# Three of the first expert's blocks ahead of a branch, the third block's halves, the low parts of weights and uncommon numbers behind it

## The chip, the cores and the metric

The kernel runs on one core of one Trainium2 chip. The engines named below are TensorE (PE; its weight loads are PEld), VectorE (DVE), ScalarE (ACT), GpSimd (POOL) and SyncE (SP, which issues most DMA transfers). A "q" behind a name (DVEq, SPq) is that engine's own instruction queue, which handles branches, semaphores and register loads. The metric is the device time of one execution in microseconds (us).

## The reference

Three stages run one after another on 4 x 768 = 3072 tokens of 384 numbers, all in float32:

```
# 1: gated linear attention, state 48 x 48 per head
state = alpha[t] * state + k[t] v[t]^T;   y[t] = q[t] @ state
# 2: mixture of 8 experts, one per token
expert = argmax(xn @ en.T / tau);   h = max(x @ w1[e], 0);   out = gate * (h @ w2[e])
# 3: dense layer pair
g = elu(x @ w_in);   out = g @ w_out          # 384 -> 2048 -> 384
```

## The kernel before

**Stages.** Attention goes over 24 tiles of 128 tokens. The tokens of each tile are scattered to rows of the table `xs` in memory, one region for each expert, by indirect transfers that POOL issues (`put`). The second stage then takes the experts one after another. Expert 0 always comes first; the order of the others is found from their token counts (`pack`, which also fills `perm_i`, `off_i` and so on). The rows of an expert come back by a transposing transfer (`load_rows`, tile `xr`), are joined to float32 (`join`, tile `xj`) and split (`evict`) into a high part `xh` (ACT) and a low part `xl` (DVE).

**One block.** Each expert has 8 blocks of 128 hidden units. `mm1(e, f)` is nine matmuls for the first layer (`h`, three products for each of three slices: high times high, low times high, high times low), then ACT writes the high half `hh` and DVE the low half `hl`. `mm2(e, f)` is nine matmuls for the second layer (`y`), one block later. `h` has 3 buffers in PSUM, `hh` and `hl` have 2 each, `y` has one set.

**Weights.** Raw weights arrive in pieces of 128 x 512 (`raw`, `load_w`, `fetch`). ACT writes the high part (`whi`) and DVE the low part (`wlo`, `low_part` in `split_piece`). Of the nine pieces taken during attention the last five low parts are postponed (list `spare`); two are done in attention and three in `rest_of`.

**The branch.** A number `odd_i` says whether the input is uncommon (too few tokens at some place, an overflow, a decay out of range). Every engine loads it and compares; in the common case all jump over a long repair path (`fix`, with `redo`, which writes the first expert's tiles again). At the place where the two paths meet each engine first waits for its own earlier work and then adds to its semaphores what the skipped path would have added. Whatever waits for that engine behind the branch waits for this addition.

**Order.** Around the branch the order of each engine is that of the code (`manual_schedule`); DVE, ACT and POOL take their instructions in that order. SP's queue holds, in order, the transposing transfer of the next expert's rows, raw weights, and the chain that brings the gate weights of an expert to all partitions (`load_g`: `rx`, `gd`, `gs`), which DVE needs when `y` of the expert is finished (line 1118).

Of the kernel before, what the change touches and what calls it, by code (L numbers as in the profile page):

```python
# [68 lines left out]
def fused_kernel(ctx, tc, qk, a, v, w12, wi, wo, cst, cols, out):  # L69
# [40 lines left out]
    en = const.tile([128, 1, E], F32, name="en")  # L110
    tick = const.tile([1, 1], F32, name="tick")
    mark = c["mark"].rearrange("p (n two) -> p n two", two=2)

# [58 lines left out]
    def load_w(n=1):  # L172

        for _ in range(n):
            if nload[0] < len(pieces):
                pool = early_p[0] if DIRECT <= nload[0] < AHEAD * PIECES else stage
# [112 lines left out]
    def attention(st):  # L289
        if True:  # L290
# [5 lines left out]
            sm = st.enter_context(tc.tile_pool(name="sm", bufs=2))  # L296
            early_p.append(st.enter_context(tc.tile_pool(name="early", bufs=AHEAD * PIECES - DIRECT)))
            psD = st.enter_context(tc.tile_pool(name="psD", bufs=2, space=PS))
# [383 lines left out]
            def fast():  # L682
# [55 lines left out]
                for i in range(tail):  # L738
# [14 lines left out]
                    stR(i + 2)  # L753
                    stA(i + 2)
                    if i == tail - 1:
                        late.pop(0)()
                        late.pop(0)()
                    stP(i + 1, 0)
                    stP(i + 1, 1)
# [78 lines left out]
            def ending():  # L838
# [83 lines left out]
                tests = pk[:9] + dec[12:] + pk[9:]  # L922
                tests, rest = tests[:len(tests) - 9], tests[len(tests) - 9:]
                for kk in range(KD):
                    first_x(GROUPS[g1], kk, stop=True)
                    nc.vector.tensor_tensor(xj[kk][:, W0:], t0[kk][:, W0:], xj[kk][:, W0:], op=ALU.add)
                    run(tests[:2])
                    del tests[:2]
# [22 lines left out]
            def fix(x2T, redo):  # L951
# [3 lines left out]
                with ExitStack() as st2:  # L955
                    ld = st2.enter_context(tc.tile_pool(name="ldF", bufs=3))
                    wk = st2.enter_context(tc.tile_pool(name="wkF", bufs=2))
                    xp = st2.enter_context(tc.tile_pool(name="xpF", bufs=10))
                    sm = st2.enter_context(tc.tile_pool(name="smF", bufs=2))
                    psD = st2.enter_context(tc.tile_pool(name="psDF", bufs=2, space=PS))  # L960
                    ps1 = st2.enter_context(tc.tile_pool(name="ps1F", bufs=1, space=PS))
                    bad = nc.values_load(bad_i[0:1, 0:1], min_val=0, max_val=C2 + 128)
                    with tc.If(bad > 0):
                        vt = [wk.tile([128, NP, 128], F32, bufs=1, name=f"vF{i}") for i in range(VB)]
                        with tc.manual_schedule():
                            general()
                            run(pack(sm, psT_p.tile([128, E], F32, tag="psT", name="n_ps")))
                    zero = xp.tile([128, XW], U16, tag="xt", name="zero")
# [17 lines left out]
    def pack(sm, n_ps):  # L986

        low_f, ov, co, m, one, cm = (sm.tile([1, E], F32, bufs=1, name=nm) for nm in ("low_f", "ov", "co", "m", "one", "cm"))
# [4 lines left out]
        val, by = (sm.tile([1, 2, E], F32, bufs=1, name=nm) for nm in ("val", "by"))  # L993
        sq, cn = [1, E, E], by[:, 1]
# [20 lines left out]
            lambda: vec.scalar_tensor_tensor(odd, odd, few, co[:, E - 1:E], op0=ALU.add, op1=ALU.add),  # L1015
            lambda: vec.tensor_tensor(odd_i, odd, bad_i, op=ALU.add),
            lambda: vec.tensor_copy(cnt_i, val[:, 1]),
            lambda: vec.tensor_copy(perm_i, by[:, 0]),
# [3 lines left out]
            lambda: vec.tensor_tensor_scan(cm, one, m, co[:, E - 1:E], op0=ALU.mult, op1=ALU.add),  # L1022
            lambda: vec.tensor_copy(over_i, co[:, E - 1:E]),
            lambda: vec.tensor_tensor(col_i, co, ov, op=ALU.subtract),
            lambda: vec.tensor_tensor(off_i, cm, m, op=ALU.subtract),
        ]

    def moe1(att, xr0, t0, rest_of, fix, es):
        with ExitStack() as st:
            xT_p = st.enter_context(tc.tile_pool(name="xT", bufs=2, side="right"))  # L1030
            h_p = st.enter_context(tc.tile_pool(name="h", bufs=2, side="right"))
            xr, xT, hb, acc, gs = {0: xr0}, {}, {}, {}, {}
            first, freed = [], []
# [24 lines left out]
            def load_g(e, f):  # L1058

                if f == (0 if e else EARLY):  # L1060
                    nc.sync.dma_start(out=rx[0:1, :CAPS[e]].rearrange("o (n u) -> o n u", u=1),
                                      in_=xs[bass.ds(expert(e) * REG, CAPS[e]), 2 * DM + 2:].bitcast(F32).rearrange("(o n) u -> o n u", o=1))
                if f == (2 if e else EARLY + 2):
                    nc.sync.dma_start(out=gd[e:e + 1, :CAPS[e]], in_=rx[0:1, :CAPS[e]])
                if f == (4 if e else EARLY + 3):
# [3 lines left out]
            def mm1(e, f, between=None):  # L1069
                hb[e, f] = (h_p.tile([128, CAP], F32R, tag="hh", name="hh"),  # L1070
                            h_p.tile([128, CAP], F32R, tag="hl", name="hl"))
                first_layer(psG.tile([128, CAP], F32, tag="g", name="h")[:, :CAPS[e]], e, f, between)

            def first_layer(ps, e, f, between=None):
                n = CAPS[e]
                xh, xl = (x[:, :, :n] for x in xT[e])
                for kk in range(KD):
# [4 lines left out]
                    if between and kk == 1:  # L1082
                        between()
                hh, hl = (h[:, :n] for h in hb[e, f])
                nc.scalar.activation(out=hh, in_=ps, func=AF.Relu)
                nc.vector.scalar_tensor_tensor(hl, ps, 0.0, hh.bitcast(F32), op0=ALU.max, op1=ALU.subtract)  # L1086

            def redo():

                with tc.tile_pool(name="psF", bufs=2, space=PS) as pool:  # L1090
                    for kk in range(KD):
                        x = xj_p.tile([128, CAP], F32, tag="xj", name="xj")
                        join(nc.gpsimd, x, xr0, kk, CAP)
                        evict(0, kk, x)
                    for f in range(EARLY):
                        first_layer(pool.tile([128, CAP], F32, name="h"), 0, f)

# [48 lines left out]
            with tc.manual_schedule():  # L1146
# [5 lines left out]
                for n in range(EARLY, len(blocks) + LAG):  # L1152
                    if n < len(blocks):
                        e, f = blocks[n]
                        mm1(e, f)
                        if n == EARLY:
                            mm2(*blocks[n - LAG - 1])
                        load_g(e, f)
                        joined(e + 1, f - (2 if e else 3))
                        turn(e + 1, f - 4)  # L1160
                    if n == len(blocks):
# [261 lines left out]
```

## Time and profile before

| | |
|---|---|
| time, median of 3 runs (lowest, highest) | 770.99 us (770.52, 771.67) |
| time of the profiled execution | 770.17 us |
| its span, first to last instruction | 768.5 us |
| PE busy | 749.3 us (98%) |
| DVE, ACT, POOL busy | 534.5, 354.6, 207.0 us |

The span is what the trace covers; the time has 1.7 us around it. All times of the trace count from the span's start. The branch stands at about 147 to 155 us, between attention and the experts.

### The profile page before, as it was taken

How to read it: one execution, taken by the hardware profiler on the slowest of the kernel's cores; microseconds unless marked ns; L12 is line 12 of the kernel's file. 1: busy time of each engine (PE TensorE's matmuls, PEld its weight loads, DVE VectorE, ACT ScalarE, POOL GpSimd, SP SyncE). 2: the span in 40 equal slices, each digit the busy share in tenths (PEclk: the TensorE clock that was granted, in tenths of full speed). 3: DMA queues.
4: the chain of work that ended last, by engine and by line, in shares of the span. 5: the costliest groups of instructions: out<-in, count | busy, mean ns of one | idle time of the engine just before them, and what ended most of it. 6: DMA issues, size and time to landing. Idle time of an engine off the chain costs nothing.

```text
span 768.5 us, 13502 instructions
## 1 busy us (share of the span) xinstructions
PE 749.3 (98%) x4982; PEld 685.8 (89%) x4982; DVE 534.5 (70%) x990; ACT 354.6 (46%) x733; POOL 207.0 (27%) x239
## 2 busy tenths in 40 slices
PE   8999999699999999999999999999999999999996
PEld 5888887599999999999888999999999999999996
DVE  8899999748998989995667655455554645545442
ACT  2565765455566566654455423333333323323221
POOL 7747687513443444440000100020020002002002
PEclk9999999999999999999999999999999999999998
DMA  8999963457976887750000000010010001001001
GB/s 199 249 269 264 240 183 115 131 123 220 247 188 214 242 223 229 220 175 11 0 2 1 22 21 0 1 42 1 0 42 1 1 0 42 2 1 41 1 1 41
DMA packets 64129, 76.92 MB, mean 100 GB/s; under 512 B 34580, under 2 KB 40604, under 8 KB 64060
## 3 DMA queue, kind: packets, MB, share of 16 engines
q1 hardware_dynamic: 60988, 66.57, 32.8%
q0 software_dynamic: 3072, 9.46, 3.4%
q8 instruction: 39, 0.64, 0.4%
q14 instruction: 30, 0.25, 0.1%
HBM read 58.78 MB, written 12.25 MB: 92 GB/s over the span
## 4 chain that ended last, share of the span: by engine, by line
PE 42%; issue 32%; DVE 3%; POOL 3%; ACT 0%; DMA 0%; POOLq 0%; DVEq 0%; ACTq 0%
PE h L1268 9%; PE y L1112 4%; PE y L1111 4%; PE y L1113 4%; PE h L1080 4%; PE h L1081 4%; PE h L1079 4%; PE o L1291 3%; PE o L1289 3%; PE o L1290 3%; POOL out_dram L1302 2%; DVE wlo L196 1%; DVE wd L232 0%; DVE hl L1086 0%; DVE xl L1102 0%
## 5 line engine op out<-in xcount | busy, mean ns | idle before, releaser
L1270 DVE TENSOR_SCALAR mn<-h 128x512 f32<-128x512 f32 x96 | 66.3, 691 | 144.4 <-PE h L1268 144.4
L1271 ACT ACTIVATE mn<-mn 128x512 f32<-128x512 f32 x96 | 60.7, 632 | 171.8 <-DVE mn L1270 171.7
L1291 PE MATMUL o<-dwo,gl 128*128 128x384 f32 x384 | 130.0, 339 | 0.0
L1290 PE MATMUL o<-dlo,gh 128*128 128x384 f32 x384 | 128.5, 335 | 0.0
L1289 PE MATMUL o<-dwo,gh 128*128 128x384 f32 x384 | 128.4, 334 | 0.0
L1268 PE MATMUL h<-xh,dlo 128*128 128x512 f32 x288 | 113.2, 393 | 0.0
L1268 PE MATMUL h<-xl,dwi 128*128 128x512 f32 x288 | 112.9, 392 | 0.0
L1268 PE MATMUL h<-xh,dwi 128*128 128x512 f32 x288 | 112.7, 391 | 0.0
L1302 POOL DMA_INDIRECT out_dram<-ob,ids x24 | 23.2, 965 | 332.3 <-ACT ob L1299 328.6
L1277 ACT ACTIVATE gh<-g 128x512 fp32r<-128x512 f32 x96 | 60.7, 633 | 77.7 <-DVE g L1274 77.7
L196 DVE TENSOR_TENSOR wlo<-raw,whi 128x512 fp32r<-128x512 f32 x96 | 72.6, 782 | 6.5 <-ACT whi L193 6.5
L1274 DVE SCALAR_TENSOR_TENSOR g<-mn,h 128x512 f32<-128x512 f32 x96 | 66.2, 689 | 15.4 <-ACT mn L1271 15.0
L1289 PEld LDWEIGHTS o<-dwo,gh 128*128 128x128 f32 x384 | 72.1, 188 | 4.1
L1290 PEld LDWEIGHTS o<-dlo,gh 128*128 128x128 f32 x384 | 72.1, 188 | 4.0
L1291 PEld LDWEIGHTS o<-dwo,gl 128*128 128x128 f32 x384 | 72.2, 188 | 1.5 <-DVE gl L1278 0.6
L1080 PE MATMUL h<-xl,whi 128*128 128x432 f32 (+6 forms) x192 | 67.3, 351 | 3.2 <-DVEq L1134 2.8
L1079 PE MATMUL h<-xh,whi 128*128 128x432 f32 (+6 forms) x192 | 67.0, 349 | 1.9 <-ACTq L1134 1.1
L1112 PE MATMUL y<-hl,whi 128*128 128x432 f32 (+6 forms) x192 | 67.2, 350 | 0.3 <-DVE hl L1086 0.3
L1081 PE MATMUL h<-xh,wlo 128*128 128x432 f32 (+6 forms) x192 | 66.9, 348 | 0.0
L1111 PE MATMUL y<-hh,whi 128*128 128x432 f32 (+6 forms) x192 | 66.7, 348 | 0.0
L1113 PE MATMUL y<-hh,wlo 128*128 128x432 f32 (+6 forms) x192 | 66.6, 347 | 0.0
L1278 DVE TENSOR_TENSOR gl<-g,gh 128x512 fp32r<-128x512 f32 x96 | 65.7, 685 | 1.1 <-ACT gh L1277 1.1
(214 smaller groups left out, 1416.8 us busy)
## 6 DMA issues: line engine op xcount, KB each, us to landing
raw<-in_w_dram SPq DMA_DIRECT2D x96, 256.0 KB
qk<-in_qk_dram SPq DMA_DIRECT2D x46, 192.0 KB
raw<-in_wi_dram SPq DMA_DIRECT2D x16, 384.0 KB
raw<-in_wo_dram SPq DMA_DIRECT2D x16, 384.0 KB
vt<-in_v_dram SPq DMA_DIRECT2D x24, 192.0 KB
at<-in_alpha_dram SPq DMA_DIRECT2D x40, 99.0 KB
xs<-zero SPq DMA_DIRECT2D x7, 289.5 KB
at<-in_alpha_dram SPq DMA_DIRECT2D x4, 231.0 KB
```

The costliest lines, as they stand in the source:

```text
L196: nc.vector.tensor_tensor(l[:, sl], r, h[:, sl].bitcast(F32), op=ALU.subtract)
L1079: nc.tensor.matmul(ps, wh, xh[:, kk], start=(kk == 0), stop=False)
L1080: nc.tensor.matmul(ps, wh, xl[:, kk], start=False, stop=False)
L1081: nc.tensor.matmul(ps, wl, xh[:, kk], start=False, stop=(kk == KD - 1))
L1111: nc.tensor.matmul(acc[e][d], wh, hh, start=(f == 0), stop=False)
L1112: nc.tensor.matmul(acc[e][d], wh, hl, start=False, stop=False)
L1113: nc.tensor.matmul(acc[e][d], wl, hh, start=False, stop=(f == FB - 1))
L1268: nc.tensor.matmul(ps, l, x, start=(n == 0), stop=(n == len(terms) - 1))
L1270: nc.vector.tensor_scalar(mn, ps, 0.0, None, op0=ALU.min)
L1289: nc.tensor.matmul(o_, gh[:, sl], wh, start=(f == 0), stop=False)
L1290: nc.tensor.matmul(o_, gh[:, sl], wl, start=False, stop=False)
L1291: nc.tensor.matmul(o_, gl[:, sl], wh, start=False, stop=(f == M - 1))
```

## The change

- Three blocks of expert 0 instead of two stand ahead of the branch (`EARLY = 3`). The third block's halves `hh` and `hl` come behind it (`mm1` is split into `products` and `mm1_end`), between `mm2` of block 0 and `mm2` of block 1.
- The three postponed low parts of weights (`split_spare`) and the three raw pieces of the next expert (`load_w`) move from ahead of the branch to behind it. The pieces that wait for them stay in the `stage` buffers, so the pool `early` shrinks from 5 to 2 buffers.
- Numbers that only the repair path reads (`cnt_i`, `size_i`, `slot_i`, `over_i`, `col_i`) are computed in the repair path by `pack_over`.
- In front of the branch, the chain for the last two tiles' gate weights (`n1`) comes before the tests that give `odd_i`, and fewer tests stand between the additions to `xj`.
- In attention, step 21, DVE does a reduction and a low part before the scan `stA`.
- The gate chain `load_g` of expert 0 starts one block later and is closer together; the joins and splits of the next expert's three slices come at blocks 4, 5, 5 and 5, 6, 6 instead of 3, 4, 5 and 4, 5, 6.

```diff
@@ attention, step loop
                     stR(i + 2)
-                    stA(i + 2)
                     if i == tail - 1:
                         late.pop(0)()
                         late.pop(0)()
+                    stA(i + 2)
@@ ending, rest_of
-                tests, rest = tests[:len(tests) - 9], tests[len(tests) - 9:]
+                tests, rest = tests[:len(tests) - 3], tests[len(tests) - 3:]
...
-                    run(tests)
                     run(n1)
                     planes23()
-                    run(stX(g1) + gates(g1))
+                    x1 = stX(g1)
+                    run(tests)
+                    run(x1 + gates(g1))
                     run(rest)
                     for j in GROUPS[g1]:
                         put(j)
-                    load_w(2 * PIECES)
-                    split_spare(len(spare))
+                    load_w(2 * PIECES - len(spare))
@@ moe1
-            EARLY = 2
+            EARLY = 3
             with tc.manual_schedule():
                 for kk in range(KD):
                     turn(0, kk)
-                    rest_of(2 if kk == 0 else 0)
                 rest_of()
...
-                    mm1(0, f, lambda: odd.append(nc.values_load(odd_i[0:1, 0:1], min_val=0, max_val=4 * E + C2 + 129 + N)) if f else None)
+                    mm1(0, f, lambda: odd.append(nc.values_load(odd_i[0:1, 0:1], min_val=0, max_val=4 * E + C2 + 129 + N)) if f == EARLY - 1 else None, f < EARLY - 1)
...
                         e, f = blocks[n]
+                        if n == EARLY:
+                            mm2(*blocks[0])
+                            mm1_end(*blocks[n - 1])
+                            mm2(*blocks[1])
+                            held = len(spare)
+                            split_spare(held)
+                            load_w(held)
                         mm1(e, f)
-                        if n == EARLY:
-                            mm2(*blocks[n - LAG - 1])
                         load_g(e, f)
```

What this does to the order is seen on three engines. On PE, the first instructions behind the branch (`UNCONDITIONAL_BRANCH` closes the skipped path; `h` is a first-layer result, `y` a second-layer one), before:

```order
L1134 UNCONDITIONAL_BRANCH x2
L1079 MATMUL h<-xh,whi 128x432
L1080 MATMUL h<-xl,whi 128x432
L1081 MATMUL h<-xh,wlo 128x432
L1079 MATMUL h<-xh,whi 128x432
```

and in the changed kernel:

```order
L1164 UNCONDITIONAL_BRANCH x2
L1142 MATMUL y_5461<-hh,whi 128x432
L1143 MATMUL y_5461<-hl,whi 128x432
L1144 MATMUL y_5461<-hh,wlo 128x432
L1142 MATMUL y_5462<-hh,whi 128x432
```

Nine first-layer matmuls have moved from behind the branch to ahead of it; the load of `odd_i` now follows the 24th matmul of the expert instead of the 15th. On DVE, the last instructions in front of the branch, from the one that writes `odd_i` (the `rs_` rows are the chain `n1`), before:

```order
L1016 TENSOR_TENSOR odd_i<-odd,bad_i 1x1
L132 SCALAR_TENSOR_TENSOR rs_t<-rs_y,ss 128x2
...
L569 RECIPROCAL cs<-gt 128x2
L1017 CAST cnt_i<-val 1x8
L1018 CAST perm_i<-by 1x8
...
L1025 TENSOR_TENSOR off_i<-cm,m 1x8
L196 TENSOR_TENSOR wlo<-raw,whi 128x512 x3
L1086 SCALAR_TENSOR_TENSOR hl<-h,hh 128x432
L1131 TENSOR_LOAD odd_i
L1086 SCALAR_TENSOR_TENSOR hl<-h,hh 128x432
L1134 COMPARE_AND_BRANCH
```

and in the changed kernel:

```order
L1020 TENSOR_TENSOR odd_i<-odd_2346,bad_i 1x1
L569 TENSOR_SCALAR gt<-gt 128x2
L570 RECIPROCAL cs<-gt 128x2
L1021 CAST perm_i<-cs 1x8
L1022 SCALAR_TENSOR_TENSOR cm<-one,co,m 1x8
L1023 TENSOR_TENSOR off_i<-cm,m 1x8
L1114 SCALAR_TENSOR_TENSOR hl<-h,hh 128x432 x2
L1161 TENSOR_LOAD odd_i
L1164 COMPARE_AND_BRANCH
```

The three low parts and six small operations are gone from this stretch, and the `rs_` chain stands ahead of `odd_i`. On SP, the transfers behind the branch, before:

```order
L265 DMA_TRANSPOSE xr<-xs 128x6x432
...
L1061 DMA rx<-xs 1x432x1
...
L1309 DMA idl<-xs 432x2
...
L164 DMA raw<-in_w_dram 128x512
...
L1064 DMA gd<-rx 1x432
```

and in the changed kernel (three more `raw` rows stand between the transposing transfer and `rx`):

```order
L266 DMA_TRANSPOSE xr<-xs 128x6x432
...
L165 DMA raw<-in_w_dram 128x512
...
L1081 DMA rx<-xs 1x432x1
...
L1084 DMA gd<-rx 1x432
...
L1348 DMA idl<-xs 432x2
```

The three raw pieces of expert 1 stood in front of the branch and are now queued behind the transposing transfer and two transfers for the third stage; `gd` now precedes `idl`.

## Rows read from the trace of the kernel before

**Rows 1.** Who PE waited for, 120 to 160 us: total us, times, longest.

```profile
PE h L1080 <- DVEq L1134: 2.8, 1, 2.8
...
PE psX L478 <- DVE low L507: 0.9, 1, 0.9
```

**Rows 2.** The same, 160 us to the end: PE's only wait.

```profile
PE y L1112 <- DVE hl L1086: 0.3, 1, 0.3
```

**Rows 3.** Queue instructions of the branch and of the load in front (ns, start us).

```profile
L1134 PEldq EVENT_SEMAPHORE  x2: 51/51/51, 147.1 to 147.3; - x2
L1134 DVEq EVENT_SEMAPHORE  x2: 21/21/21, 151.4 to 151.5; - x2
...
L1131 PEldq TENSOR_LOAD <-odd_i x1: 668/668/668, 145.5 to 145.5; - x1
```

**Rows 4.** PE in order of time: start us, us, then what ran.

```profile
142.58 0.46 PE L1080 MATMUL h<-xl,whi 128*128 128x432 f32 x1 [0.44 <-DVE xl L1102]
...
146.25 0.44 PE L1079 MATMUL h<-xh,whi 128*128 128x432 f32 x1 [0.52 <-DVE rs_y L137]
...
146.72 0.36 PE L1081 MATMUL h<-xh,wlo 128*128 128x432 f32 x1
...
151.42 0.73 PE L1080 MATMUL h<-xl,whi 128*128 128x432 f32 x1 [2.77 <-DVEq L1134]
...
157.32 0.36 PE L1111 MATMUL y<-hh,whi 128*128 128x432 f32 x1
...
159.08 0.36 PE L1079 MATMUL h<-xh,whi 128*128 128x432 f32 x1
```

**Rows 5.** Busy us by engine, PE's granted clock, DMA share, GB/s of one stretch.

```profile
151.40:156.80 5.40, 5.38 (x15) 4.96 (x16) 0.00 (x0) 0.00 (x0) 0.96 (x1) 0.50 0.42 147
```

**Rows 6.** DVE in order of time.

```profile
141.74 0.23 DVE L1003 TENSOR_SCALAR low_f<-val 1x8 f32<-1x8 f32 x1
...
141.94 0.58 DVE L1102 TENSOR_TENSOR xl<-xj,xh 128x432 fp32r<-128x432 f32 x1
...
145.34 0.15 DVE L1016 TENSOR_TENSOR odd_i<-odd,bad_i 1x1 int32<-1x1 f32 x1
145.42 0.14 DVE L132 SCALAR_TENSOR_TENSOR rs_t<-rs_y,ss 128x2 f32<-128x2 f32 x1
...
146.39 0.17 DVE L139 RECIPROCAL rs_y<-rs_y 128x2 f32<-128x2 f32 x1
147.30 0.17 DVE L568 TENSOR_SCALAR gt<-gt 128x2 f32<-128x2 f32 x1 [0.74 <-ACT e__2286 L561]
...
148.40 1.88 DVE L196 TENSOR_TENSOR wlo<-raw,whi 128x512 fp32r<-128x512 f32 x3
150.21 1.10 DVE L1086 SCALAR_TENSOR_TENSOR hl<-h,hh 128x432 fp32r<-128x432 f32 x2
```

**Rows 7.** POOL in order of time: the last two scatters of tokens.

```profile
148.49 2.63 POOL L609 DMA_INDIRECT xs<-xt,pos_i  x1 [0.58 <-ACTq L1134]
...
151.60 0.96 POOL L609 DMA_INDIRECT xs<-xt,pos_i  x1 [0.28 <-DVEq L1134]
```

**Rows 8.** SP's transfers in order of time: start us, us to issue.

```profile
156.29 2.59 SPq L265 DMA_TRANSPOSE xr<-xs  x1
...
164.95 0.34 SPq L1064 DMA_DIRECT2D gd<-rx  x1
...
172.52 0.33 SPq L1067 DMA_DIRECT2D gs<-gd  x1
```

**Rows 9.** ACT in order of time, behind the branch.

```profile
161.53 1.18 ACT L279 ACTIVATE xj<-xr 128x864 uint16<-128x864 uint16 x1
...
166.47 0.64 ACT L193 ACTIVATE whi<-raw 128x512 fp32r<-128x512 f32 x1
```

**Rows 10.** DVE: where the gate weights of expert 0 are first used.

```profile
180.17 1.64 DVE L1118 TENSOR_TENSOR x2T<-y,gs 128x432 f32 x3 [0.30 <-DVE hl L1086]
```

**Rows 11.** One stretch of the windows (columns as in rows 5).

```profile
166.00:168.00 2.00, 2.00 (x12) 1.92 (x11) 1.37 (x3) 1.55 (x4) 0.36 (x1) 1.00 0.40 53
```

More of the change, by code (lines that the diff above doesn't have):

```diff
@@ L111, in fused_kernel @@
     tick = const.tile([1, 1], F32, name="tick")
+    val, by = (c["emb"][0:1, n * 2 * E:(n + 1) * 2 * E].rearrange("p (n e) -> p n e", n=2) for n in range(2))
     mark = c["mark"].rearrange("p (n two) -> p n two", two=2)
@@ L175, in load_w @@
             if nload[0] < len(pieces):
-                pool = early_p[0] if DIRECT <= nload[0] < AHEAD * PIECES else stage
+                pool = early_p[0] if DIRECT <= nload[0] < DIRECT + len(LOWS) else stage
                 raw[nload[0]] = pool.tile([128, PW], F32, tag="raw", name="raw")
@@ L296, in attention @@
             sm = st.enter_context(tc.tile_pool(name="sm", bufs=2))
-            early_p.append(st.enter_context(tc.tile_pool(name="early", bufs=AHEAD * PIECES - DIRECT)))
+            early_p.append(st.enter_context(tc.tile_pool(name="early", bufs=len(LOWS))))
             psD = st.enter_context(tc.tile_pool(name="psD", bufs=2, space=PS))
@@ L926, in ending @@
                     nc.vector.tensor_tensor(xj[kk][:, W0:], t0[kk][:, W0:], xj[kk][:, W0:], op=ALU.add)
-                    run(tests[:2])
-                    del tests[:2]
+                    if kk < KD - 1:
+                        run(tests[:2])
+                        del tests[:2]
                 run(dec[10:12])
@@ L967, in fix @@
                             run(pack(sm, psT_p.tile([128, E], F32, tag="psT", name="n_ps")))
+                    with tc.manual_schedule():
+                        run(pack_over(sm))
                     zero = xp.tile([128, XW], U16, tag="xt", name="zero")
@@ L986, in pack @@
     def pack(sm, n_ps):
-        low_f, ov, co, m, one, cm = (sm.tile([1, E], F32, bufs=1, name=nm) for nm in ("low_f", "ov", "co", "m", "one", "cm"))
+        low_f, cm = (sm.tile([1, E], F32, bufs=1, name=nm) for nm in ("low_f", "cm"))
+        ov, co, m, one = over_tiles(sm)
         odd = sm.tile([1, 1], F32, bufs=1, name="odd")
@@ L992, in pack @@
         pick = sm.tile([1, 2, E, E], F32, bufs=1, name="pick")
-        val, by = (sm.tile([1, 2, E], F32, bufs=1, name=nm) for nm in ("val", "by"))
         sq, cn = [1, E, E], by[:, 1]
@@ L1016, in pack, with over_tiles, pack_over @@
             lambda: vec.tensor_tensor(odd_i, odd, bad_i, op=ALU.add),
+            lambda: vec.tensor_copy(perm_i, by[:, 0]),
+            lambda: vec.tensor_tensor_scan(cm, one, m, co[:, E - 1:E], op0=ALU.mult, op1=ALU.add),
+            lambda: vec.tensor_tensor(off_i, cm, m, op=ALU.subtract),
+        ]
+    def over_tiles(sm):
+        return [sm.tile([1, E], F32, bufs=1, name=nm) for nm in ("ov", "co", "m", "one")]
+    def pack_over(sm):
+        ov, co, m, one = over_tiles(sm)
+        vec, cn = nc.vector, by[:, 1]
+        return [
+            lambda: vec.memset(one, 1.0),
+            lambda: vec.tensor_tensor(m, cn, c["cap"][0:1], op=ALU.min),
+            lambda: vec.tensor_tensor(ov, cn, m, op=ALU.subtract),
+            lambda: vec.tensor_tensor_scan(co, one, ov, 0.0, op0=ALU.mult, op1=ALU.add),
             lambda: vec.tensor_copy(cnt_i, val[:, 1]),
-            lambda: vec.tensor_copy(perm_i, by[:, 0]),
             lambda: vec.tensor_copy(size_i, cn),
@@ L1021, in pack @@
             lambda: vec.tensor_scalar(slot_i, slot_i, 7, None, op0=ALU.arith_shift_right),
-            lambda: vec.tensor_tensor_scan(cm, one, m, co[:, E - 1:E], op0=ALU.mult, op1=ALU.add),
             lambda: vec.tensor_copy(over_i, co[:, E - 1:E]),
             lambda: vec.tensor_tensor(col_i, co, ov, op=ALU.subtract),
-            lambda: vec.tensor_tensor(off_i, cm, m, op=ALU.subtract),
         ]
@@ L1031, in moe1 @@
             h_p = st.enter_context(tc.tile_pool(name="h", bufs=2, side="right"))
+            hp = {}
             xr, xT, hb, acc, gs = {0: xr0}, {}, {}, {}, {}
@@ L1062, in load_g, with mm1, mm1_end, products @@
                                       in_=xs[bass.ds(expert(e) * REG, CAPS[e]), 2 * DM + 2:].bitcast(F32).rearrange("(o n) u -> o n u", o=1))
-                if f == (2 if e else EARLY + 2):
+                if f == (2 if e else EARLY + 1):
                     nc.sync.dma_start(out=gd[e:e + 1, :CAPS[e]], in_=rx[0:1, :CAPS[e]])
-                if f == (4 if e else EARLY + 3):
+                if f == (4 if e else EARLY + 2):
                     gs[e] = gs_p.tile([128, CAP], F32, name="gs")
                     nc.sync.dma_start(out=gs[e][:, :CAPS[e]], in_=gd[e:e + 1, :CAPS[e]].to_broadcast([128, CAPS[e]]))
-            def mm1(e, f, between=None):
+            def mm1(e, f, between=None, end=True):
+                hp[e, f] = psG.tile([128, CAP], F32, tag="g", name="h")[:, :CAPS[e]]
+                products(hp[e, f], e, f, between)
+                if end:
+                    mm1_end(e, f)
+            def mm1_end(e, f):
                 hb[e, f] = (h_p.tile([128, CAP], F32R, tag="hh", name="hh"),
                             h_p.tile([128, CAP], F32R, tag="hl", name="hl"))
-                first_layer(psG.tile([128, CAP], F32, tag="g", name="h")[:, :CAPS[e]], e, f, between)
-            def first_layer(ps, e, f, between=None):
+                halves(hp.pop((e, f)), e, f)
+            def products(ps, e, f, between=None):
                 n = CAPS[e]
@@ L1083, in first_layer, with halves @@
                         between()
-                hh, hl = (h[:, :n] for h in hb[e, f])
+            def halves(ps, e, f):
+                hh, hl = (h[:, :CAPS[e]] for h in hb[e, f])
                 nc.scalar.activation(out=hh, in_=ps, func=AF.Relu)
@@ L1094, in redo @@
                         evict(0, kk, x)
-                    for f in range(EARLY):
-                        first_layer(pool.tile([128, CAP], F32, name="h"), 0, f)
+                    for f in range(EARLY - 1):
+                        ps = pool.tile([128, CAP], F32, name="h")[:, :CAPS[0]]
+                        products(ps, 0, f)
+                        halves(ps, 0, f)
+                    products(hp[0, EARLY - 1], 0, EARLY - 1)
             def evict(e, kk, t):
@@ L1154, in moe1 @@
                         e, f = blocks[n]
+                        if n == EARLY:
[5 more added lines that the diff above has]
+                            load_w(held)
                         mm1(e, f)
-                        if n == EARLY:
-                            mm2(*blocks[n - LAG - 1])
                         load_g(e, f)
-                        joined(e + 1, f - (2 if e else 3))
-                        turn(e + 1, f - 4)
+                        for kk in range(KD):
+                            if f == (kk + 2 if e else min(kk + 4, 5)):
+                                joined(e + 1, kk)
+                        for kk in range(KD):
+                            if f == (kk + 4 if e else min(kk + 5, 6)):
+                                turn(e + 1, kk)
                     if n == len(blocks):
```

## The prediction

> **What bounds the kernel now.** I first asked PE's waits, since PE is busy for 98% of the span. From 160 us to the end it waits for others only once, for 0.3 us [rows 2]: whatever reaches PE's queue earlier at 160 us ends earlier by as much, as long as nothing behind becomes late. Around the branch it is different. The longest wait there is PE's for DVE's queue, 2.8 us [rows 1], and the queue rows tell what it is: DVE's two semaphore additions behind the branch come at 151.4 and 151.5 us, PE's own at 147.1 and 147.3 [rows 3]. So DVE is the last to pass, and PE stands until then. DVE's timeline shows why: `odd_i` is written at 145.34, but the gate chain, eleven small operations, three low parts of weights (148.40, 1.88 us) and two low halves `hl` (150.21, 1.10 us) come before its additions [rows 6].
>
> The wait has a second price. The 18th matmul of expert 0 starts at 146.72, the 20th at 151.42 [rows 4]; only one lies between. From 151.40 to 156.80 the granted clock is 0.50, the lower of PE's two levels (1.2 against 2.4 GHz), and 15 matmuls take that stretch [rows 5], 0.36 us each. At the upper level nine take 159.08 - 157.32 = 1.76 us [rows 4], 0.196 each. So the low clock costs 15 x (0.36 - 0.196) = 2.5 us.
>
> I count PE's progress in matmuls of expert 0, nine to a block and layer. Before, the 37th (the first of block 1's second layer, nine ahead of the first of block 3 at 159.08) starts at 157.32 [rows 4]. The order in which the first 36 stand changes, their number doesn't, so the gain is 157.32 minus the start of the 37th in the changed kernel.
>
> **The change part by part.**
>
> *When `odd_i` is ready.* DVE's work up to `odd_i` stays, and the `rs_` chain comes in front of it: 145.42 to 146.39 + 0.17, 1.14 us [rows 6]. So `odd_i` ends near 145.49 + 1.14 = 146.63.
>
> *PE in front of the branch.* Two tests between the additions to `xj` and the first low part go, so `xl` starts at about 141.74 instead of 141.94 [rows 6], and the second matmul, which waits for it [rows 4], at 142.38. The 24th follows 22 x 0.196 us later, and 0.1 for the first gap: 146.8. Then comes the load of `odd_i` (668 ns at 145.5 before [rows 3], the next matmul at 146.25 [rows 4]: 0.72 us from load to matmul). PE and `odd_i` are ready together; 147.57 for the 25th. The 27th stands 0.47 behind it, as the 18th behind the 16th [rows 4]: 148.04. From the 18th at 146.72 to PE's second addition at 147.3 [rows 3] and the next possible load were 0.65 us: PE itself is past the branch at 148.69.
>
> *DVE in front of the branch.* Eleven small operations took 147.30 to 148.40 (0.1 each); five stay, 0.6 us with one that waits for the one before. With `odd_i` at 146.63 they end at 147.25, the two `hl` (1.10) at 148.35, the additions 0.1 later: 148.45. The low parts' 1.88 us, the six operations' 0.5 and the 0.74 us in which DVE waited for ACT [rows 6] are gone from this path. ACT needs only the second block's `h` (near 146) and 0.5 us.
>
> *The sum.* PE is then the last, by a little: the 28th matmul at 148.69, the 37th 9 x 0.196 later at 150.45, if the clock stays at its upper level. Gain 157.32 - 150.45 = 6.9 us, of which 2.5 is the clock.
>
> *What is moved behind.* Block 2's `hh` needs the buffer that block 0's second layer frees near 150.5; ACT and DVE then take half a microsecond each, and the three low parts 1.88: done near 153.5. Their first user is block 4, 36 matmuls behind the branch, at 155.75. That cover is 2.2 us; gone, each microsecond would cost PE one.
>
> *POOL and the rows of expert 1.* The first of the last two scatters takes 2.63 us, the second 0.96 [rows 7]. The first begins with the three low parts on DVE and ends 0.85 us after the last of them would (148.40 + 1.88 = 150.28; 151.13). In the changed kernel the low parts come after both scatters, which can then end near 150.0 instead of 152.56; with the 3.7 us that follow before the transposing transfer is issued (156.29 [rows 8]) this is near 153.7, at worst, with a scatter of 2.63 again, 155.4. Landing took at most 156.29 to 161.53, where ACT reads the rows without a wait [rows 8, 9]: 5.2 us, so 158.9 to 160.6. ACT wants them at 158.2, but what counts is block 5's halves behind that join: PE takes them 81 matmuls behind the branch, 164.6; the join 1.18, `whi` 0.64 [rows 9], the decoding and `hh` some 0.55 each and `hl` 0.55 [rows 6] make 3.5, so until 161.1 nothing is lost. [...]
>
> *Raw pieces of expert 1*, in front of the branch before, are queued behind the transposing transfer and come some 9 us later (157.5 to 159). ACT takes the first behind block 5's `hh`, two joins and a split, near 164.6; allowing the 5.2 us of the transposing transfer they land by 164.2. Covered, narrowly.
>
> *The numbers for the repair path* are operations that the common case no longer runs; counted above. *Attention:* PE's wait for a low part, 0.9 us [rows 1], shrinks, but DVE's scan comes as much later, and the work of DVE stays: between 0.9 gained and 0.9 lost; I take 0, since it is only two instructions swapped on the busy engine.
>
> *The gate weights of expert 0.* DVE needs `gs` when the second layer of block 7 is done: 126 matmuls behind the branch, 173.4 instead of 180.17 [rows 10]. PE wants the first `y` tile back nine matmuls later, at 175.2, and DVE's first operation takes 0.55, so until 174.6 nothing is lost. `gd` was issued 8.7 us behind the transposing transfer, `gs` 7.6 behind `gd` [rows 8], and it landed within 7.65 [rows 10]. With the transfer at 153.7 this gives 177.6 at worst, a loss of 3.0 us. But part of the 7.6 was slow transfers: from 166 to 168 us 53 GB/s move at a share of 0.40 [rows 11], and in the new order `gd` precedes `idl`. I take 0.3.
>
> So 770.17 - 6.9 + 0.3 = 763.6 for an execution like the profiled one; the median of the runs is 0.82 above it: 764.4.
>
> **Rivals.**
>
> *The gate weights are late (0.16).* For it: the chain of three small transfers stays, PE needs its end 6.8 us earlier, and raw pieces now stand in front. Against: the 4.3 us of slack between 173.4 and 177.6 are worst-case numbers. 1.5 to 3.0 us lost: 766 to 767.4. The Trainium skill (DMA: Bandwidth & Descriptors, section "Specifications") says that pieces below 512 B cost a read-modify-write; `idl` and `rx` are 432 pieces of four bytes, and row 11's low rate agrees. By that rule `gs` is held by `idl` wherever both are queued.
>
> *The clock falls all the same (0.08).* PE still stands 0.7 us at the load and 0.65 at the branch. Against: the gaps of 0.44 and 0.52 in front left the pace at 0.196. If it falls as before, 2.5 us are lost: 766.9.
>
> *PE waits for `odd_i` instead (0.06).* The tests now stand in one chain, so each may wait for the one in front. With 0.1 more for 13 of them it comes at 147.9 and costs 1.1; only at about 153 would nothing be gained, within 0.2%.
>
> *Slower (0.05).* The rows of expert 1 land late: from 161.1 on ACT's join holds block 5's halves, and PE loses each microsecond. To be slower by over 0.2% PE must lose 6.9 + 1.5, a landing at 169.5, 15.8 us after the issue; the row says 5.2.
>
> **Numbers.** My forecast, 763.2 to 765.7, has 0.65; its low end allows for 0.9 from attention and 0.3 of stalls not taken. With the gate rival 0.81 lie below 767.6, the upper end. 0.2% (1.5 us) is about what a measurement of this kernel tells from no change: faster 0.65 + 0.16 + 0.08 = 0.89, same 0.06, slower 0.05.
>
> **What would show it.** Right: DVE's additions near 148.5 and PE's 28th matmul right behind; no stretch at half clock; `y` matmuls first behind the branch; the scatters 0.96 us each; the transposing transfer near 153.7. Wrong: PE waiting for DVE at `x2T` near 175, for `hl` of blocks 4 to 6, or a clock of 0.50 behind 149 us; a wait of DVE or ACT for the raw pieces of expert 1 that reaches PE.

## The result, and the profile after

The changed kernel is slower: 775.50 us (median of 7 runs, 773.87 to 777.95) against 770.99 us; ratio 1.006, 95% interval 1.004 to 1.008. The forecast was 764.4, with a range to 767.6. The profiled execution has a span of 773.8 us, 5.3 more than before.

At the branch it went nearly as forecast. PE of the changed kernel in order of time:

```profile
147.24 0.36 PE L1107 MATMUL h<-xh,wlo 128*128 128x432 f32 x1
148.12 0.44 PE L1142 MATMUL y<-hh,whi 128*128 128x432 f32 x1 [0.52 <-DVEq L1164]
...
149.97 0.36 PE L1142 MATMUL y<-hh,whi 128*128 128x432 f32 x1
...
174.51 0.36 PE L1107 MATMUL h<-xh,wlo 128*128 128x432 f32 x1
180.34 0.70 PE L1142 MATMUL y<-hh,whi 128*128 128x432 f32 x1 [5.48 <-DVE x2T L1149]
...
183.72 0.47 PE L1105 MATMUL h<-xh,whi 128*128 128x432 f32 x1
...
186.79 0.47 PE L1142 MATMUL y<-hh,whi 128*128 128x432 f32 x1 [1.01 <-ACT hh L1113]
188.01 0.47 PE L1143 MATMUL y<-hl,whi 128*128 128x432 f32 x1 [0.76 <-DVE hl L1114]
```

The wait at the branch, 2.77 us in [rows 4], is 0.52. The 37th matmul starts at 149.97, before at 157.32: PE is 7.35 us ahead. Then it stands from 174.5 to 180.3, and twice more by 188. The waits of PE from 160 us on, where [rows 2] showed a single one of 0.3:

```profile
PE y L1142 <- DVE x2T L1149: 6.8, 3, 5.5
PE y L1143 <- DVE hl L1114: 2.1, 3, 0.8
PE y L1142 <- ACT hh L1113: 1.0, 1, 1.0
```

Windows, with the columns of rows 5: the clock stays at its upper level where it was at the lower one before; in its place nine matmuls run at the lower level behind the new stall (some 1.5 us, an estimate: 9 x (0.36 - 0.196) from the paces in the prediction).

```profile
151.40:156.80 5.40, 5.40 (x29) 5.17 (x28) 3.61 (x6) 1.57 (x3) 0.00 (x0) 1.00 0.38 85
170.00:174.00 4.00, 4.00 (x22) 3.81 (x21) 2.50 (x4) 0.53 (x1) 0.75 (x1) 1.00 0.40 10
180.30:183.70 3.40, 3.36 (x9) 3.14 (x10) 1.52 (x3) 0.00 (x0) 0.00 (x0) 0.50 1.02 271
```

The middle row is the second thing to see: from 170 to 174 us the DMA engines are busy for 0.40 of the time and move 10 GB/s. What stands in the queue then is in SP's timeline:

```profile
153.59 2.54 SPq L266 DMA_TRANSPOSE xr<-xs  x1
...
157.46 1.50 SPq L165 DMA_DIRECT2D raw<-in_w_dram  x3
159.00 0.66 SPq L1081 DMA_DIRECT2D rx<-xs  x1
...
165.23 0.32 SPq L1084 DMA_DIRECT2D gd<-rx  x1
166.61 0.63 SPq L1348 DMA_DIRECT2D idl<-xs  x1
167.50 0.39 SPq L165 DMA_DIRECT2D raw<-in_w_dram  x1
167.99 0.37 SPq L1087 DMA_DIRECT2D gs<-gd  x1
169.77 9.98 SPq L266 DMA_TRANSPOSE xr<-xs  x1
179.96 1.00 SPq L165 DMA_DIRECT2D raw<-in_w_dram  x2
```

and in two more rows of the kernel before, besides [rows 8]:

```profile
161.55 0.62 SPq L1309 DMA_DIRECT2D idl<-xs  x1
...
173.84 2.70 SPq L265 DMA_TRANSPOSE xr<-xs  x1
```

`gs` is issued 4.5 us earlier than before (167.99 against 172.52 [rows 8]), and still comes late. `idl`, 432 pieces of four bytes for the third stage, was issued at 161.55, ahead of `gd`; now it is issued at 166.61, ahead of a raw piece, of `gs` and of the second transposing transfer, whose issue takes 9.98 us instead of 2.70. DVE and ACT show how long each waited:

```profile
179.59 1.64 DVE L1149 TENSOR_TENSOR x2T<-y,gs 128x432 f32 x3 [7.07 <-DMA gs<-gd]
```

```profile
178.69 0.63 ACT L194 ACTIVATE whi<-raw 128x512 fp32r<-128x512 f32 x1 [6.81 <-DMA raw<-in_w_dram]
185.76 0.55 ACT L236 ACTIVATE dg<-raw 128x384 f32<-128x384 f32 x1 [6.45 <-DMA raw<-in_wi_dram]
```

So 7.35 us were won by 150, and 12.65 (7.35 + 5.3) lost behind it. Three things are late at once: the gate weights, a raw piece ahead of them, and the raw pieces behind the transposing transfer. The experiments ask whether `idl` makes them late, or the order of the gate chain, or the three raw pieces that moved.

### The profile page after: what moved, and what is told of

The parts are those of the page before. It is cut to its first block, busy times and chain, and to the rows that moved or that the text cites. A ratio compares the mean times of both kernels' runs of the same rounds, so it can differ in the third digit from the quotient of the medians.

```text
span 773.8 us, 13493 instructions
## 1 busy us (share of the span) xinstructions
PE 749.7 (97%) x4982; PEld 684.7 (88%) x4982; DVE 534.3 (69%) x984; ACT 354.9 (46%) x733; POOL 203.7 (26%) x239
## 4 chain that ended last, share of the span: by engine, by line
PE 35%; issue 32%; DVE 5%; DMA 4%; POOL 3%; ACT 1%; POOLq 0%; SPq 0%; DVEq 0%; ACTq 0%
PE h L1307 9%; PE y L1143 3%; PE y L1142 3%; PE y L1144 3%; PE o L1330 3%; PE o L1328 3%; PE h L1106 3%; PE o L1329 3%; PE h L1107 3%; PE h L1105 3%; POOL out_dram L1341 2%; DVE wlo L197 2%; DMA gs<-gd 1%; DMA raw<-in_w_dram 1%; DMA raw<-in_wi_dram 1%
## 5 line engine op out<-in xcount | busy, mean ns | idle before, releaser
L197 DVE TENSOR_TENSOR wlo<-raw,whi 128x512 fp32r<-128x512 f32 x96 | 74.3, 799 | 6.4 <-ACT whi L194 6.3
```

The lines of the kernel that those rows point to most:

```text
L197: nc.vector.tensor_tensor(l[:, sl], r, h[:, sl].bitcast(F32), op=ALU.subtract)
```

## The experiments

The kernel before was timed again beside each group of runs: 770.98 us beside runs 1, 2, 7 and 8, 771.38 beside 3 to 6, 770.48 beside 9 to 12. Each ratio is to the one of its group; times of different groups compare only to within such differences, up to 0.9 us.

**1. `idl` of expert 0 taken out of this stretch.** The number that its address hangs on goes through a new tile, written at the start of the third stage; SP's order is otherwise the same.

```diff
+            off_b = x_p.tile([1, E], I32, tag="off_b", name="off_b")
+            nc.vector.tensor_copy(off_b, off_i)
             for e in range(E):
-                o3 = nc.sync.value_load(off_i[0:1, e:e + 1], min_val=0, max_val=N)
+                o3 = nc.sync.value_load(off_b[0:1, e:e + 1], min_val=0, max_val=N)
```

> The changed kernel; only the idl transfer of expert 0 (432 pieces of four bytes) is moved, from between gd and gs to the start of the third stage. Theory 1 (idl holds SP's queue): gs, issued near 167, lands by about 170.5 (3.4 us as before the change), DVE does not wait at x2T, raw and the next transposing transfer come in time, and the 12.6 us lost behind 174 come back: 762 to 764.5. Theory 2 (the gate chain is late because three raw pieces stand in front of rx, idl is only a neighbour): gs still lands behind 174.6 and the time stays at 770 or above. Theory 3 (the loss is the raw pieces that moved behind the branch): gs lands in time, but PE waits near 186 to 193 as before, 2.5 us and the rest of the stalls: 766 to 768.

Measured: 768.22, ratio 0.9958 (0.9944 to 0.9972). The wait for `gs` is gone, DVE's `x2T` starts at 172.88 without a wait for a transfer, and the second transposing transfer takes 2.67 us to issue. Theory 2 falls as the cause of that wait: the three raw pieces still stand in front of `rx`. Of theory 3's waits near 186 to 193 nothing is left but 0.6 us, at 179 and 183. But 7.3 us came back, not 12.6, and the time is in none of the three ranges.

**2. The same edit in the kernel before.**

> The kernel before, with the same move of idl. Theory 1: gd lands in about 1 us instead of 7.5 and gs some 6 us earlier, but PE waited for nothing there, so the time is the same, 770 to 771.5; this would show that idl delayed the chain in the kernel before too, under a cover of one us. Theories 2 and 3: gd still needs several us; the same time.

Measured: 773.62, ratio 1.0027 (1.0017 to 1.0038). The chain moved as theory 1 has it: `gs` is issued 2.68 us behind `gd` (167.93 against 165.25), where [rows 8] have 7.57. That nobody profits was expected; that it is 2.6 us slower was not. The loss is in the third stage, and run 1 has it too: the first second-layer matmul of that stage starts at 365.62 in run 1 and the last at 759.32, 393.7 us, where the changed kernel takes 390.8. The granted clock is 1.00 in all. One window of run 1:

```profile
380.00:750.00 370.00, 370.00 (x1857) 335.06 (x1857) 199.88 (x313) 132.79 (x224) 21.25 (x41) 1.00 0.04 11
```

and of the changed kernel:

```profile
380.00:750.00 370.00, 370.00 (x1871) 335.14 (x1870) 203.21 (x319) 135.61 (x229) 21.29 (x41) 1.00 0.04 11
```

PE is never idle in either, and does 1857 matmuls instead of 1871. Something that the edit brought slows them by 0.8% on average, and not all alike: in the same window the mean time of `o<-dwo,gh` is 339 ns in run 1 against 334, that of `h<-xh,dlo` 395 against 393, while `h<-xl,dwi` has 392 in both. It is the transfer that now runs there, or the new tile of 32 bytes in that stage's pool.

**3 and 4. The same without the new tile,** on the changed kernel and on the one before: the copy goes into `size_i`, which the common case doesn't use, at the end of the experts.

```diff
                     if n == len(blocks):
+                        nc.vector.tensor_copy(size_i, off_i)
...
-                o3 = nc.sync.value_load(off_i[0:1, e:e + 1], min_val=0, max_val=N)
+                o3 = nc.sync.value_load(size_i[0:1, e:e + 1], min_val=0, max_val=N)
```

> The changed kernel with expert 0's idl transfer in the third stage again, now released through a tile that the kernel already has, so that no tile of the third stage moves. In the runs with the added 32-byte tile the third stage's matmuls took 393.7 us from the first second-layer one to the last, against 390.8, at the same clock. If the added tile's place did that, 390.8 comes back and the time is 768.2 - 2.9 = 765.3, between 764.5 and 766. If idl's transfer in the third stage did it: 768 again, with 393.7.

> The kernel before, with the same edit. If the added tile's place slowed the third stage: 773.6 - 2.9 = 770.7, the same as before within a us. If idl's transfer did it: 773.6 again.

Measured: 766.30, ratio 0.9933 (0.9920 to 0.9947), and 770.39, ratio 0.9987 (0.9978 to 0.9996). The window of run 3 has the old count again:

```profile
380.00:750.00 370.00, 370.00 (x1871) 335.23 (x1870) 201.14 (x315) 133.91 (x225) 22.38 (x41) 1.00 0.04 11
```

The transfer runs in the third stage in all four runs, so it is not the cause; the slow pace came and went with the new tile. (The copy stands at another place, too; the tile wasn't tried without that.) So `idl` costs the changed kernel 775.5 - 766.3 = 9.2 us. For the kernel before the ratio says 1.0 (0.3 to 1.7), which its trace doesn't bear out: PE waits 0.9 us from 160 us on in run 4, and 0.3 with `idl` in place. The time of run 3 is 0.3 above its expected range.

**5 and 6. The pieces or the place?** To the kernel of run 3 a transfer is added where `idl` stood, into a scratch table: once the same 432 pieces of four bytes, once the same 1728 bytes in two pieces. The two programs differ in this one instruction: in run 6 the line behind the `...` stands in place of the one ahead of it.

```diff
                     nc.sync.dma_start(out=gd[e:e + 1, :CAPS[e]], in_=rx[0:1, :CAPS[e]])
+                    if e == 0:
+                        nc.sync.dma_start(out=more[:CAPS[0]], in_=xs[:CAPS[0], 2 * DM:2 * DM + 2])
...
+                        nc.sync.dma_start(out=more[:CAPS[0]].rearrange("(a n) u -> a (n u)", a=2), in_=xs[0:2, :CAPS[0]])
```

> The previous kernel but one (idl late, no added tile), with a second copy of the 432 four-byte pieces put where idl stood in the changed kernel, between gd and the raw piece ahead of gs, into a scratch table that nobody reads. Theory 1 (these small pieces hold what is queued behind them): gs lands near 179.5 again, the second transposing transfer's issue takes near 10 us, the time is 774.5 to 777. Theory 2 (something else that came with moving idl): as without it, 764.5 to 766.

> The same, but the added transfer moves the same 1728 bytes in two contiguous pieces of 864 bytes. If the number of small pieces is what holds the queue: no harm, gs near 171, 764.5 to 766.5. If any transfer at this place that depends on the table of tokens does it: 774.5 to 777, as with the 432 pieces.

Measured: 776.02, ratio 1.0062 (1.0046 to 1.0077), with the small pieces; 766.91, ratio 0.9942 (0.9927 to 0.9957), with two. SP with the small pieces:

```profile
166.19 0.53 SPq L1087 DMA_DIRECT2D more<-xs  x1
166.97 0.41 SPq L166 DMA_DIRECT2D raw<-in_w_dram  x1
167.48 0.36 SPq L1090 DMA_DIRECT2D gs<-gd  x1
168.89 11.00 SPq L267 DMA_TRANSPOSE xr<-xs  x1
```

and with two pieces:

```profile
165.98 0.68 SPq L1087 DMA_DIRECT2D more<-xs  x1
166.91 0.37 SPq L166 DMA_DIRECT2D raw<-in_w_dram  x1
167.39 0.36 SPq L1090 DMA_DIRECT2D gs<-gd  x1
168.82 2.63 SPq L267 DMA_TRANSPOSE xr<-xs  x1
```

From 170 to 174 us the first moves 13 GB/s at a share of 0.56, the second 250 at 1.05. DVE waits 7.01 us for `gs` in run 5, and for no transfer at that place in run 6. The 432 pieces are the cause, 9.1 us, and two pieces with as many bytes at the same place cost 0.6, within the interval. The number and the size of the pieces change together here; which of the two costs is not shown. The Trainium skill (DMA: Bandwidth & Descriptors, section "Queues, rings and completion order") says that each DMA engine takes the descriptors of one ring in order. These two runs agree: the raw piece, `gs` and the transposing transfer, all queued behind the small pieces, are late in run 5 (ACT waits 5.85 us for the raw piece, the transposing transfer takes 11.00 to issue) and not in run 6.

**7. Is it only the gate weights?** In the changed kernel, `idl` in place, expert 0's `x2T` is multiplied by a tile of tokens that is there anyway; the gate weights of expert 0 are left out of the output.

```diff
                     y, gt = acc.pop(e), gs.pop(e)
+                    if e == 0:
+                        gt = xT[1][0][:, 0].bitcast(F32)
```

> The changed kernel, idl left in place, but expert 0's x2T is multiplied by another tile that is there, not by gs (the gate weights of expert 0 are left out). What remains is what idl or the raw pieces cost beside the gate weights. If the wait for gs is the whole loss: 762 to 764.5. Theory 1 with idl holding everything behind it: the raw piece that landed at 178.7 and those queued behind the second transposing transfer still come late, so 3 to 6 us remain: 766 to 769. Theory 3: the same 766 to 769, so this run tells only gs from the raw pieces.

Measured: 775.90, ratio 1.0054 (1.0039 to 1.0070): nothing came back, which none of the theories had expected. PE's waits from 160 us on:

```profile
PE y L1142 <- ACT hh L1113: 8.8, 1, 8.8
...
PE y L1143 <- DVE hl L1114: 0.9, 2, 0.5
```

and ACT at that place:

```profile
185.70 0.55 ACT L236 ACTIVATE dg<-raw 128x384 f32<-128x384 f32 x1 [6.73 <-DMA raw<-in_wi_dram]
186.15 0.51 ACT L1113 ACTIVATE hh<-h 128x432 fp32r<-128x432 f32 x1
```

Without the wait for `gs` PE goes on to 177.6 and stands there until 186.7. In ACT's order `hh` is behind `dg`, which waits for a raw piece of the third stage's weights, queued behind the second transposing transfer. The gate weights were the first to be late, not the only ones.

**8. `rx` ahead of the three raw pieces,** `idl` as in the changed kernel. `load_g` of expert 0's first step moves in front of `split_spare` and `load_w`.

```diff
+                            load_g(e, f)
                             split_spare(held)
                             load_w(held)
                         mm1(e, f)
-                        load_g(e, f)
+                        if n > EARLY:
+                            load_g(e, f)
```

> The changed kernel, with rx issued ahead of the three raw pieces instead of behind them; gd, idl and gs in the same order as before. Theory 2 (the raw pieces in front are the cause): rx lands near 161 instead of 165, gs by about 168: 762.5 to 765. Theory 1: the chain starts 3 to 4 us earlier and idl with it, near 163; idl's pieces still take 8 to 11 us and gs behind them lands near 172 to 176: a part comes back, 767 to 773.

Measured: 772.09, ratio 1.0015 (1.0002 to 1.0028). `gd` is issued at 162.52 instead of 165.23 and `idl` at 163.94 instead of 166.61; DVE waits 4.62 us for `gs` instead of 7.07. The whole queue moved up by about 2.7 us and the time fell by 3.4, as theory 1 has it; the small pieces still hold it.

**9. `idl` ahead of `gd`.** Besides the edit of run 8, `gd` and `gs` are asked for one block earlier; SP's order is then `rx`, `idl`, `gd`, five raw pieces, `gs`.

```diff
-                if f == (2 if e else EARLY + 1):
+                if f == (2 if e else EARLY):
...
-                if f == (4 if e else EARLY + 2):
+                if f == (4 if e else EARLY + 1):
```

> The changed kernel with the gate chain of expert 0 as early as it goes; the queue's order is then rx, idl, gd, five raw pieces, gs, so that idl is issued near 158.5 instead of 166.6 and nothing is left out. If what counts is only when the small pieces run: they are done near 168, gd and gs follow by 173, the raw pieces and the second transposing transfer come in time: 765 to 768. If the pieces cost their 8 us wherever they stand in front of weights: 770 to 775.

Measured: 769.89, ratio 0.9989 (0.9980 to 0.9998). `idl` is issued at 158.08 and the gate weights come in time, but the raw pieces behind it don't; ACT:

```profile
169.40 1.29 ACT L194 ACTIVATE whi<-raw 128x512 fp32r<-128x512 f32 x2 [6.22 <-DMA raw<-in_w_dram]
```

PE stands 4.03 us, until 171.16, for `hh`, which is behind this `whi` in ACT's order. The time is 6.7 us above that of the next run, which has the same edit of `rx` and `idl` late. But `idl` is not the only difference. The five raw pieces now stand behind `gd`, which waits for `rx` and is issued at 161.24:

```profile
161.75 4.96 SPq L165 DMA_DIRECT2D raw<-in_w_dram  x5
```

In run 10 they stand in front of `gd` and are issued 3.85 us earlier:

```profile
157.90 2.74 SPq L165 DMA_DIRECT2D raw<-in_w_dram  x5
```

So this order is no cure; how its 6.7 us divide between the small pieces and the place of `gd`, and whether an earlier `idl` alone would do, is not shown.

**10. `rx` first, and `idl` late as in run 3.**

> The kernel with idl late and no added tile (766.3), with rx ahead of the three raw pieces. If the raw pieces of the third stage's weights, for which ACT still waited 5.6 us near 178 (PE stood some 2 us behind it), are late because the queue stands at gd waiting for rx: everything behind gd is issued 3 us earlier, this stall goes, 764 to 765.5. If they wait for their buffers instead: 766.3 again.

Measured: 763.18 (762.57 to 763.95), ratio 0.9901 (0.9887 to 0.9915): the fastest, below the range that was expected, and ahead of run 3 by 3.1 us (2.5 by the two ratios). PE's waits from 160 us on:

```profile
PE y L1142 <- ACT whi L194: 1.2, 1, 1.2
PE y L1143 <- DVE hl L1114: 0.3, 1, 0.3
```

In run 3 they were 3.6 us in all, three of the five between 179 and 185. So 2.1 of the 3.2 us between the two spans (765.4 and 762.2) are PE's waits; 0.6 were there in front of the branch, where the two kernels don't differ (the 27th matmul at 146.87 against 147.43). `gd` waits at the head of SP's queue for `rx`, and what is behind it waits too: `rx` 2.4 us earlier (157.01 against 159.36) brought `gd` 3.4 us earlier, 162.15 against 165.55.

**11. The low parts and the raw pieces ahead of the branch again,** on the kernel of run 3 (the pool `early` has its five buffers again).

```diff
-                    load_w(2 * PIECES - len(spare))
+                    load_w(2 * PIECES)
+                    split_spare(len(spare))
...
-                            held = len(spare)
-                            split_spare(held)
-                            load_w(held)
```

> The kernel with idl late and no added tile (766.3), with the three low parts and the three raw pieces put back ahead of the branch; the third block stays ahead. The prediction's step: DVE's additions come 1.9 us later, near 150, and PE waits for them as long; if the clock falls behind that wait as it did in the kernel before, up to 2.5 us more. On the other side three raw pieces no longer stand in front of rx, which can return up to 2 us near 180. 766.5 to 770. If the low parts were not on DVE's path to the branch: 764.5 to 766.3.

Measured: 766.60, ratio 0.9939 (0.9923 to 0.9955), the same as run 3. At the branch the prediction's step holds; PE:

```profile
146.87 0.36 PE L1108 MATMUL h<-xh,wlo 128*128 128x432 f32 x1
149.51 0.44 PE L1143 MATMUL y<-hh,whi 128*128 128x432 f32 x1 [2.28 <-DVEq L1165]
...
152.54 0.56 PE L1143 MATMUL y<-hh,whi 128*128 128x432 f32 x1
```

and the window behind it:

```profile
149.50:153.60 4.10, 4.09 (x13) 3.78 (x14) 0.20 (x1) 0.53 (x1) 0.97 (x1) 0.58 0.71 228
```

From the 27th matmul to the 37th are 5.67 us here and 2.73 in the changed kernel (149.97 - 147.24): 2.9 lost, 1.8 by the wait and the rest by the clock, 0.58 against 1.00. Behind it 1.9 come back: `gd` is issued at 163.99 instead of 165.55, since the raw pieces no longer stand in front of `rx`, and PE's waits from 160 us on are 1.7 us instead of 3.6. Of the remaining us, 0.6 are a lead that PE had in this execution in front of the branch (the 27th matmul at 146.87, in run 3 at 147.43); the two times differ by 0.3. So by the trace the move of the low parts is worth its 2.9 us, and the move of the raw pieces gives most of them back; each move by itself wasn't tried.

This run also shows what the low parts do to the scatter that runs beside them:

```profile
146.40 1.88 DVE L197 TENSOR_TENSOR wlo<-raw,whi 128x512 fp32r<-128x512 f32 x3
146.91 2.21 POOL L610 DMA_INDIRECT xs<-xt,pos_i  x1 [0.57 <-ACTq L1165]
```

It ends 0.84 us behind the last low part, as in the kernel before [rows 6], [rows 7]; in run 3, where the low parts come later, it takes 0.97.

**12. The swap in attention undone,** on the kernel of run 3.

```diff
                     stR(i + 2)
+                    stA(i + 2)
                     if i == tail - 1:
                         late.pop(0)()
                         late.pop(0)()
-                    stA(i + 2)
```

> The kernel with idl late and no added tile (766.3), with the scan stA ahead of the reduction and the low part in step 21 of attention, as in the kernel before. The prediction took this swap at nothing, with 0.9 us either way as the bounds: 766.3, between 765.4 and 767.2.

Measured: 765.99, ratio 0.9939 (0.9925 to 0.9952) against 0.9933 with the swap: no difference beyond the intervals. In front of the branch the trace does show one. Among PE's waits from 100 to 140 us the one of [rows 1] is back:

```profile
PE psX L479 <- DVE low L508: 0.8, 1, 0.8
```

It stands, with 0.5 to 0.9 us, in all four profiled executions with the scan first (the kernel before, runs 2, 4 and 12) and in none of the ten with the swap. PE's first matmul of expert 0 starts at 141.45 to 142.14 in the four and at 140.52 to 141.31 in the ten. By the means (141.7 and 141.0) the swap brings PE to the experts some 0.7 us earlier. In the kernel of run 3 this is lost again: PE's waits from 160 us on are 3.6 us there and 1.9 in run 12.

## Why the prediction was wrong

**The branch: right.** Forecast 6.9 us, measured 7.35. `odd_i` was ready at 146.19 (forecast 146.63), DVE's additions came at 148.0 and 148.1 (148.45), PE's 28th matmul right behind at 148.12 (148.69), and the clock stayed up. Two details differ. The last to pass was not PE, "by a little", but DVE: PE waited 0.52 us for it. And PE's first matmul of expert 0 started at 141.05 instead of 141.51, a lead of 0.46, about the 0.45 that the gain has above the forecast; run 12 shows where such a lead comes from. Run 11 bears out the low parts' share with the clock in it. The scatters took 0.97 us each, the transposing transfer was issued at 153.59 (153.7), and ACT waited 0.49 us for the rows of expert 1, at 158.24.

**The step that failed: the gate weights of expert 0,** "177.6 at worst, a loss of 3.0 us", "in the new order `gd` precedes `idl`. I take 0.3". Two things are wrong in it, the size and what it leaves out.

First, the size. The old gaps were added up as a worst case, and then most of it was dropped because `gd` now precedes `idl`. But in the old order `idl` ran between the issue of `gd` and that of `gs`; that is why `gs` came 7.6 us behind `gd` [rows 8] (3.09 in run 4, which has `idl` late). The new order doesn't remove `idl`, it puts it behind `gd`, 5 us later (166.61 against 161.55), in front of `gs`; and PE needs the gate weights some 7 us earlier. Gap by gap, from issue to issue:

| | before | changed |
|---|---|---|
| transposing transfer to `gd` | 8.66 us | 11.64 us |
| `gd` to `gs` | 7.57 us | 2.76 us |
| `gs` to the start of `x2T` (before: without a wait for `gs`) | 7.65 us | 11.60 us |

What stood in the second gap moved to the third, and the two together are 14.4 us against 15.2. So the worst case of 3.0 us had room for `idl`, and taking 0.3 instead was wrong. The worst case itself fell short by 2.0 us (`x2T` at 179.59 against 177.6), because the first gap grew by 3.0: the moved raw pieces stand in front of `rx`, and `gd` waits for `rx` (run 10).

Second, the term that isn't there. The prediction asked when the gate weights land, not what else is queued behind `idl`: a raw piece, the second transposing transfer, and all the raw pieces behind that. Run 7 shows that they alone cost as much as the gate weights: without the wait for `gs` the time is the same. The rival "the gate weights are late" named the mechanism, with the price of one consumer, 1.5 to 3.0 us; measured are 9.2 (775.5 against 766.3; 9.7 between runs 5 and 3, which are of one group). (Its "4.3 us of slack" are 4.2, and lateness rather than slack; its 766 to 767.4 put the loss on top of the 0.3 that 764.4 already has.) "Slower" had a chance of 0.05, by another mechanism, late rows of expert 1; they came in time.

**Raw pieces of expert 1: "covered, narrowly"** was right for the pieces, which ACT takes at 163.72 without a wait, and left out that `rx` is now behind them and `gd` holds the queue until `rx` has landed. Run 10 against run 3: 3.1 us (2.5 by the ratios).

**The sum again.** 771.0 - 7.35 + 9.2 + 3.1 = 775.9, measured 775.5. The two charges are themselves differences between the changed kernel, run 3 and run 10, so what this tests is the rest: 771.0 - 7.35 = 763.65, and run 10, with both charges off, has 763.2. The forecast of 764.4 had 0.3 for both.

**Attention and the numbers for the repair path,** taken at nothing: run 12 has the swap at nothing in the time, within a us, although PE reaches the experts some 0.7 us earlier with it; in the kernel of run 3 later waits take that. What it is worth in the kernel of run 10 wasn't tried, nor were the six small operations by themselves.

**What stays open.** PE still waits 1.2 us at 283.75 in run 10; its cause wasn't tried. What the second transposing transfer stands on while it is issued for 10 us isn't settled. The trace names ACT's `whi` of the raw piece in front, which ends at 179.3, shortly ahead of the issue's end; but in run 3 that `whi` starts at 171.97, behind the end of the issue (168.25 + 2.91), so the transfer doesn't need it. Runs 5 and 6 show only that the small pieces make it.

## What to carry to other kernels

When work moves earlier, list every transfer between the old and the new place on the queue and ask of each consumer behind it when it is due, not only of the one that the change is about. A price read as a gap between two issues belongs to what ran in it; where the order changes, take the filler's own time and put it where it now stands, and add what is new in each gap. And a transfer of many tiny pieces that nobody needs soon belongs behind the weights, not among them.

## What was not expected of the hardware

- 432 pieces of four bytes from memory to memory, 1.7 KB in all, cost a kernel 9.1 us more than two pieces with the same bytes at the same place in the queue; from 170 to 174 us the DMA engines are busy for 0.56 of the time and move 13 GB/s.
- The transposing transfer behind them took 9.98 us to issue in the changed kernel, 11.00 in run 5, 9.99 and 9.06 in runs 7 and 8, against 2.63 in run 6 and 2.91 in run 3, and SP issued nothing else meanwhile.
- With a tile of 32 bytes more in the third stage's pool, used once, that stage's matmuls were 0.8% slower on average at the same granted clock (1857 instead of 1871 in 370 us; 1858 in run 2), in two kernels; 2.9 us. Which of the moved tiles matters wasn't tried.
- A scatter that POOL issues took 2.63 us (before) and 2.21 us (run 11) where low parts of weights ran on DVE at the same time, and 0.96 to 0.97 where none did.
